# Two transfers of 16 four-byte rows at the head of the load queues, and two weight loads in one piece instead of two

## The chip, the cores and the metric

The kernel runs on one core of one Trainium2 chip. The metric is the device time of one execution in microseconds (us), as the median of several runs. Beside it stands one profiled execution, from which the span (first to last instruction) and all views are taken.

## The reference, cut to what matters

One block of a diffusion transformer with an image stream (2 x 256 tokens) and a text stream (2 x 32 tokens), D = 1152, all in bf16:

```
mod_i = (silu(c) @ wmod_img).reshape(B, 6, 1, D)        # shift, scale, gate; the same for text
shi, sci, gai = mod_i[:, 0], mod_i[:, 1], mod_i[:, 2]
hi   = layernorm(x_img) * (1 + sci) + shi
qkvi = hi @ wqkv_img                                     # q, k, v in thirds of 3*D columns
...
p    = softmax(q @ k.T * D**-0.5)                        # text and image tokens joined, per batch
a    = p @ v
out_i = x_img + gai * (ai @ wo_img)
out_t = x_txt + gat * (at @ wo_txt)
```

## The kernel before, in words

The order of all work is written out by hand (`tc.manual_schedule()`): each engine runs its instructions in program order, and so does each load queue.

**Loads.** Every weight comes from HBM in row tiles of 128 partitions. SyncE's queue (SP, in the profile queue q1) carries nearly all of them, in the order of the program: `c` (L81), then the four column chunks of the image scale weight `w_sc_i` (`load_sc`, L94) with the rows of the image value weight `w_v_i` (`load_v`, L98, L110: nine row tiles `kt`, 288 KB each) and two tiles of `x_img` (`load_x`, L90) between them, and after these the other weights (`load_w`, L76). The first two of the four tiles of `x_img` are issued on ScalarE's queue (ACT, q10). `load_w` takes a tuple `ksplits`: `K3` loads a weight in three pieces, `K2` in two (kt 0 to 4, kt 5 to 8), the default in one piece. Five buffers of the pool `w` go round among the large weights; `w_ga_i` has the home "V", the place that `w_v_i` leaves.

The framework gives every transfer on the two hardware queues one of eight semaphores in turn. A transfer that gets a semaphore again waits at its issue until the one eight places before it has landed.

**First stage (0 to about 31 us).** TensorE runs 15 matmuls on zeros to warm up (L143). Meanwhile VectorE takes the layernorm statistics of x tile 0 (L169), then of tiles 1 and 2. With each scale chunk (two or three kt of columns) TensorE computes the scale columns (`mod_scale`, L223; the last chunk by `mod_scale_last`, L240 and L245), and the value projection accumulates row by row over kt (`v_row`, L282; `v_narrow`, L294) as the scale columns and the value rows arrive. The matmuls of kt 6 to 8 need the last chunk's scale.

**The rest.** The shift row, q and k of the image, the text stream, scores, softmax, attention and the output projections follow, almost without a gap on TensorE. `w_sc_t` (text scale, L460) is read by `row_strips` through `mod_strip` (L429), `w_ga_i` (image gate, L464) by `scores_txt_and_gate` (L636, L641, L657).

**The spare columns.** `xf_full` is a tile of 128 x (2*VC + 64), with VC = 288. Its view `xf` uses columns 0 to 2*VC - 1, loaded late (L812) and read at the end (L879). The columns from 2*VC on are read by nothing.

Of the kernel before, what the change touches and what calls it, by code (L numbers as in the profile page):

```python
# [14 lines left out]
def kernel(  # L15
# [14 lines left out]
    nc = tc.nc  # L30
# [4 lines left out]
    B, NI, D = x_img.shape  # L35
    NT = x_txt.shape[1]
    P = 128
# [7 lines left out]
    VC = 288  # L45
# [18 lines left out]
    xi_flat = x_img.rearrange("b n d -> (b n) d")  # L64
# [5 lines left out]
    def w_view(src):  # L70
        return src.rearrange("(kt p) n -> p kt n", p=P)

    def load_w(src, c0, ksplits=((0, KT),), home=None):
        t = wpool.tile([P, KT, D], bf, tag="w", name="t") if home is None else act.tile([P, KT, D], bf, tag=home, name="w_home")
        for (k0, k1) in ksplits:
            nc.sync.dma_start(t[:, k0:k1, :], w_view(src)[:, k0:k1, c0:c0 + D])  # L76
        return t
# [6 lines left out]
    xf_full = act.tile([P, 2 * VC + 64], bf)  # L84
# [4 lines left out]
    def load_x(i, eng=nc.sync):  # L89
        eng.dma_start(x_i[:, i, :], xi_t[:, i, :])  # L90

    def load_sc(ch):
        k0, k1 = KC[ch]
        nc.sync.dma_start(w_sc_i[:, :, k0 * P:k1 * P], w_view(wmod_img)[:, :, D + k0 * P:D + k1 * P])  # L94
# [4 lines left out]

    for i in range(TPB):  # L100
        load_x(i, nc.scalar)
    load_sc(0)
    load_x(2)
    load_v(0)
# [9 lines left out]
    K2 = ((0, 5), (5, KT))  # L114
# [342 lines left out]

    w_k_i = load_w(wqkv_img, D, K3)
    w_sh_t = load_w(wmod_txt, 0)
    w_sc_t = load_w(wmod_txt, D, K2)  # L460
    nc.sync.dma_start(x_t[0:P:P // NTT, :], xt_flat[:, :])
    w_q_t = load_w(wqkv_txt, 0, K2)
    w_k_t = load_w(wqkv_txt, D, K2)
    w_ga_i = load_w(wmod_img, 2 * D, K2, home="V")  # L464
    w_v_t = load_w(wqkv_txt, 2 * D, K3)
    w_o_i = load_w(wo_img, 0, K2)
    w_ga_t = load_w(wmod_txt, 2 * D)
# [461 lines left out]
```

## Time and profile before

| What | Value |
|---|---|
| median of 3 runs | 114.57 us (114.54 to 114.64) |
| the profiled execution's own time | 114.88 us |
| its span, first to last instruction | 113.1 us |
| TensorE matmul busy | 108.3 us, 96% of the span |
| VectorE, ScalarE, GpSimd busy | 76.1, 36.6, 28.4 us |
| bytes moved | 40.87 MB, mean 361 GB/s |
| mean granted TensorE clock | 0.997 |

The span is 1.78 us shorter than the profiled execution's own time, and that execution is 0.31 us over the median of the runs. A difference that is read from the span is therefore added to the median as it is. TensorE's 96% is an average: which engine or transfer sets the pace has to be read stage by stage.

### The profile page before, as it was taken

The page shows a single profiled execution, that of the slowest core. Times are in us where ns is not written, and L with a number is a line of the kernel's source. Part 1 is how long each engine was busy: PE and PEld are TensorE (multiplying, and loading weights), DVE is VectorE, ACT ScalarE, POOL GpSimd, SP SyncE. Part 2 cuts the span into 40 slices and gives each one's busy share as a digit, 9 for nine tenths or more (in the row PEclk, how much of TensorE's full clock was granted, in tenths as well). Part 3 has the DMA queues.
Part 4 walks back from the last instruction along what each step waited for, and adds up shares of the span by engine and source line. Part 5 has one row for each costly group of instructions (what it writes and reads, how often), then busy time and mean ns, then how long its engine had stood idle before and what let it go on. Part 6 is the DMA issues. An engine that isn't in the chain of part 4 may idle for free.

```text
span 113.1 us, 2863 instructions
## 1 busy us (share of the span) xinstructions
PE 108.3 (96%) x1195; PEld 64.0 (57%) x1204; DVE 76.1 (67%) x151; ACT 36.6 (32%) x83; POOL 28.4 (25%) x65
## 2 busy tenths in 40 slices
PE   5999999999999999999999999999999999999990
PEld 1356655555444444444446558787687556567670
DVE  1699330956399999999999950237666802995971
ACT  4537500372190071740008924025646700001000
POOL 7100120730140000000000060601550470699300
PEclk9999999999999999999999999999999999999998
DMA  3999999999999999999999999999999999994052
GB/s 92 343 333 355 375 375 405 412 411 408 407 412 412 410 411 402 413 410 412 412 411 415 408 405 407 408 392 394 407 411 397 412 408 406 371 375 161 0 191 70
DMA packets 22839, 40.87 MB, mean 361 GB/s; under 512 B 1375, under 2 KB 6635, under 8 KB 22827
## 3 DMA queue, kind: packets, MB, share of 16 engines
q1 hardware_dynamic: 21547, 39.05, 90.4%
q10 hardware_dynamic: 672, 0.77, 2.2%
q0 software_dynamic: 608, 0.88, 2.1%
q8 instruction: 9, 0.15, 0.5%
q14 instruction: 3, 0.02, 0.1%
HBM read 39.36 MB, written 1.34 MB: 360 GB/s over the span
## 4 chain that ended last, share of the span: by engine, by line
PE 80%; DMA 13%; SPq 4%; issue 1%; DVE 0%
PE qkps L529 31%; PE ps L851 16%; DMA w_sc_i<-in_wmod_img_dram 13%; PE va L282 7%; PE aps L759 5%; PE ps L590 4%; PE sps L619 4%; PE gps L429 3%; SPq L98 3%; PE ops L869 2%; PE ps L694 2%; PE van L294 1%; PE gps L824 1%; PE sps L632 1%; PE pk L703 1%
## 5 line engine op out<-in xcount | busy, mean ns | idle before, releaser
L529 PE MATMUL qkps<-hT_i,t 128*128 128x512 bf16 x158 | 35.4, 379 | 0.2
L529 PEld LDWEIGHTS <-t 128*128 128x128 bf16 x162 | 15.6, 98 | 18.7 <-issue 0.4
L491 DVE SCALAR_TENSOR_TENSOR sacc<-w_v_i,mcols,sacc 128x1152 f32<-128x1152 bf16 x16 | 22.7, 1418 | 0.5
L282 PE MATMUL va<-w_v_i,hT_i 128*128 128x512 bf16 x67 | 17.0, 379 | 0.5 <-issue 0.3
L851 PE MATMUL ps<-t,aT 128*128 128x384 bf16 x99 | 16.4, 326 | 0.0
L851 PEld LDWEIGHTS <-aT 128*128 128x128 bf16 x117 | 11.0, 98 | 6.8 <-issue 0.5
L282 PEld LDWEIGHTS <-hT_i 128*128 128x128 bf16 x72 | 6.4, 98 | 6.2 <-issue 0.2
L835 POOL TENSOR_TENSOR w_og<-t,gb 128x384 bf16<-128x384 bf16 x9 | 8.7, 999 | 4.5 <-DMA gb<-mod_scratch 4.5
L857 DVE TENSOR_TENSOR tmp<-ps,gb 128x384 bf16<-128x384 f32 x11 | 6.0, 550 | 5.6 <-DMA gb<-mod_scratch 5.0
L548 POOL TENSOR_SCALAR mod_txt<-mcols 128x18 f32<-128x18 f32 x2 | 0.6, 275 | 32.4 <-DVE mcols L435 32.4
L169 DVE BATCH_NORM_STATS2 stats<-x_i 128x6 f32<-128x384 bf16 x12 | 5.8, 541 | 2.6 <-DMA x_i<-in_x_img_dram 2.6
L143 PE MATMUL wps<-wz 128*128 128x512 bf16 x15 | 6.1, 578 | 1.2 <-DVE wz L125 1.2
L479 ACT ACTIVATE qT<-qkps 128x512 bf16<-128x512 f32 x9 | 4.7, 600 | 6.9 <-PE qkps L529 6.9
L495 ACT CAST shi<-sacc 128x1152 bf16<-128x1152 f32 x2 | 2.3, 1154 | 13.2 <-DVE sacc L491 13.2
L772 DVE TENSOR_SCALAR aT<-aps,sv 128x288 bf16<-128x288 f32 (+2 forms) x11 | 4.3, 455 | 2.0 <-PE aps L759 2.0
L590 PEld LDWEIGHTS <-t 128*128 128x128 bf16 x162 | 5.0, 98 | 0.5
L157 DVE CAST kT<-qkps 128x512 bf16<-128x512 f32 x3 | 2.1, 686 | 4.7 <-PE qkps L529 4.7
L590 PE MATMUL ps<-hT_t,t 128*128 128x64 bf16 x162 | 5.0, 193 | 0.0
L858 DVE TENSOR_TENSOR o<-tmp,x_i 128x384 bf16<-128x384 bf16 x11 | 4.7, 426 | 0.4
L759 PE MATMUL aps<-pT,v_i 128*128 128x288 bf16 (+2 forms) x44 | 4.8, 264 | 0.0
L774 ACT ACTIVATE aT<-aps,sv 128x288 bf16<-128x288 f32 (+2 forms) x11 | 4.0, 468 | 2.1 <-PE aps L759 2.1
L619 PE MATMUL sps<-kT,qT 128*128 128x288 bf16 x36 | 4.6, 286 | 0.0
(160 smaller groups left out, 139.7 us busy)
## 6 DMA issues: line engine op xcount, KB each, us to landing
t<-in_wqkv_img_dram SPq DMA_DIRECT2D x6, 864.0 KB, 13.2
t<-in_wmod_txt_dram SPq DMA_DIRECT2D x2, 2592.0 KB, 17.6
t<-in_wqkv_txt_dram SPq DMA_DIRECT2D x2, 1440.0 KB, 14.2
t<-in_wmod_img_dram SPq DMA_DIRECT2D x3, 864.0 KB, 12.3
t<-in_wqkv_txt_dram SPq DMA_DIRECT2D x3, 864.0 KB, 14.1
t<-in_wo_txt_dram SPq DMA_DIRECT2D x3, 864.0 KB, 15.5
t<-in_wqkv_txt_dram SPq DMA_DIRECT2D x2, 1152.0 KB, 15.0
w_v_i<-in_wqkv_img_dram SPq DMA_DIRECT2D x7, 288.0 KB, 6.9
```

Of the source, the lines that this page charges most:

```text
L143: nc.tensor.matmul(ps[:], lhsT=wz[:, 0:P], rhs=wz[:], start=True, stop=True)
L169: nc.vector.bn_stats(stats[0:np_, k, :], x_ap[:, k * CH:(k + 1) * CH])
L282: nc.tensor.matmul(ps[:], lhsT=hT_i[:, kt, i * P:(i + 1) * P], rhs=w_v_i[:, kt, half * VW:(half + 1) * VW], start=(kt == 0), stop=(kt == K ...
L479: nc.scalar.mul(out_ap, in_ap, SCALE)
L491: nc.vector.scalar_tensor_tensor(saccs[b][:], w_v_i[:, kt, :], ap, saccs[b][:], op0=ALU.mult, op1=ALU.add)
L529: nc.tensor.matmul(pss[j - j0][:], lhsT=wq[:, kt, j * P:(j + 1) * P], rhs=hT_i[:, kt, :], start=(kt == 0), stop=(kt == KT - 1))
L590: nc.tensor.matmul(ps[:, j - j0, :], lhsT=wq[:, kt, j * P:(j + 1) * P], rhs=hT_t[:, kt, :], start=(kt == 0), stop=(kt == KT - 1))
L619: nc.tensor.matmul(sps[:], lhsT=qkTs[0][:, ft, b, q0:q0 + P], rhs=qkTs[1][:, ft, b, :], start=(ft == 0), stop=(ft == KT - 1))
L759: nc.tensor.matmul(bank[:, off:off + c1 - c0], lhsT=lhsT, rhs=rhs, start=(first[id(bank)] == n), stop=(final[id(bank)] == n))
L835: nc.gpsimd.tensor_mul(w_og[:, dt, 0:CH], w_o_i[:, dt, NG0:D], gb[:, B - 1, NG0:D])
L851: nc.tensor.matmul(ps[:, 0:cw], lhsT=aT[:, dt, t0:t0 + P], rhs=rhs, start=(dt == DTS[0]), stop=(dt == DTS[-1]))
L857: nc.vector.tensor_mul(tmp[:, 0:cw], ps[:, 0:cw], gb[:, b, cs])
```

## The change

Two small transfers are added after the first two x tiles. One is on ScalarE's queue and reads the first two elements (4 bytes) of every 16th row of x tiles 2 and 3 (256 rows, so 16 rows). The other is on SyncE's queue, behind `c` and ahead of the first scale chunk, and reads the first two value columns of every 8th row of the first row tile of `wqkv_img` (128 rows, so 16 rows). Both write into columns of `xf_full` that nothing reads. `w_sc_t` and `w_ga_i`, which were loaded in two pieces each, are loaded in one. The number of transfers on the two hardware queues stays the same; two of them move from the middle to the head.

```diff
     for i in range(TPB):
         load_x(i, nc.scalar)
+    nc.scalar.dma_start(xf_full[0:16, 2 * VC + 2:2 * VC + 4], xi_flat[2 * P:4 * P:16, 0:2])
+    nc.sync.dma_start(xf_full[0:16, 2 * VC:2 * VC + 2], wqkv_img[0:P:8, 2 * D:2 * D + 2])
     load_sc(0)
     load_x(2)
     load_v(0)
...
     w_k_i = load_w(wqkv_img, D, K3)
     w_sh_t = load_w(wmod_txt, 0)
-    w_sc_t = load_w(wmod_txt, D, K2)
+    w_sc_t = load_w(wmod_txt, D)
     nc.sync.dma_start(x_t[0:P:P // NTT, :], xt_flat[:, :])
     w_q_t = load_w(wqkv_txt, 0, K2)
     w_k_t = load_w(wqkv_txt, D, K2)
-    w_ga_i = load_w(wmod_img, 2 * D, K2, home="V")
+    w_ga_i = load_w(wmod_img, 2 * D, home="V")
```

## The prediction

> **What bounds the kernel now.** I read the chain of waits first, then the timeline of the first 20 us, then TensorE by stage, then the two load queues in short windows around 3.6 us. The chain, from its start to 32 us:
>
> ```profile
> 0.73 0.41 SPq L81
> 1.14 0.07 issue
> 1.21 5.34 DMA w_sc_i<-in_wmod_img_dram
> ...
> 10.29 8.84 DMA w_sc_i<-in_wmod_img_dram
> 19.14 0.04 issue
> 19.18 0.57 PE sps L245 x36
> ```
>
> Columns are start, length, what. The chain starts on SyncE's queue, at the very place of the edit: issue of c, then the first scale chunk. The last scale chunk lands at 10.29 + 8.84 = 19.13 us, and L245 follows at once. From there on the chain is TensorE without a break. So a microsecond by which the last chunk lands later is paid in full at the end. TensorE by stage (start:end and length, PE busy, count, clock, DMA share, GB/s):
>
> ```profile
> 8.99:11.10 2.11, 2.06 (x15) 1.00 1.08 367
> 11.10:12.84 1.74, 1.71 (x34) 1.00 1.10 353
> 12.84:19.18 6.34, 6.23 (x55) 1.00 1.07 391
> 19.18:31.35 12.17, 11.80 (x141) 1.00 1.04 409
> 31.35:110.00 78.65, 78.44 (x907) 1.00 0.97 375
> ```
>
> TensorE is busy almost throughout from 8.99 us. A faster DMA stream has little to give; the wait that it could shorten is the one ahead of L245, and the timeline prices it:
>
> ```profile
> 18.89 0.23 PE L240 MATMUL sps<-ones_full 128*32 128x96 bf16 x4
> ...
> 19.18 0.20 PEld L245 LDWEIGHTS <-sT 128*32 128x32 bf16 x15 [0.18 <-issue]
> ```
>
> The weight loads of L245 sat 0.18 us: that is all there is to win at this place. The stage that ends here starts from x tile 0:
>
> ```profile
> 0.73 0.41 SPq L81 DMA_DIRECT2D c<-in_c_dram  x1
> 0.74 0.87 ACTq L90 DMA_DIRECT2D x_i<-in_x_img_dram  x2
> 1.21 0.42 SPq L94 DMA_DIRECT2D w_sc_i<-in_wmod_img_dram  x1
> ...
> 3.80 1.48 DVE L169 BATCH_NORM_STATS2 stats<-x_i 128x6 f32<-128x384 bf16 x3 [2.64 <-DMA x_i<-in_x_img_dram]
> ```
>
> VectorE waits for that tile and then hardly pauses until it feeds the first transposes; TensorE's value matmuls start at 9.05. That the x tile isn't loaded sooner therefore matters as much as the last chunk.
>
> **The added transfer on SyncE.** The nearest row for its issue is c, also a small transfer: 0.41 us, and 1.21 - 0.73 = 0.48 us from start to start. So the first scale chunk is issued 0.48 us later, and behind it x tile 2, the value rows and the later chunks, all on that queue. Are they covered? Later on, yes. Issues from 3.82 us on are held back by a queue that is full (two value loads take 2.49 us to issue there, 3.27 us at 6.98), and DMA is at 0.99 to 1.15 of its capacity in every window of 1 us from 5 to 19 us. A later issue costs nothing while transfers issued earlier keep the engines busy. At the head there is nothing issued earlier but the two x tiles on q10. The queues from 2.9 to 3.6 us, then from 3.6 to 4.07 us (packets, MB, share of 16 engines):
>
> ```profile
> q10 hardware_dynamic: 115, 0.24, 96.4%
> q1 hardware_dynamic: 10, 0.01, 2.4%
> ```
>
> ```profile
> q1 hardware_dynamic: 202, 0.10, 72.5%
> q10 hardware_dynamic: 39, 0.06, 32.6%
> ```
>
> Up to 3.6 us the x tiles fill the engines alone; at 3.6 us the first chunk takes over as they run out. The chunk comes when the cover ends. Bounds for the loss: nothing, if its descriptors lay ready at the engines long before and only waited behind x; all of 0.48 us, if the engines stand still for the whole shift. Between them: in the 0.47 us from 3.6 the chunk used 72.5% of the engines, 0.47 x 0.725 = 0.34 us of full DMA time, and x the rest. With the chunk shifted by that much, x still runs and the 0.34 us is lost. I take **+0.34**: 10 packets of the chunk among 115 of x from 2.9 to 3.6 say that it was only just arriving, on a few engines, and was not lying ready.
>
> The Trainium skill, in "DMA: Bandwidth & Descriptors" (Specifications), gives some 0.6 us from the issue to the first byte on the hardware queues; by that the chunk, issued by 1.63, would be there at 2.2, and 0.48 us more would still be covered by x. The trace doesn't agree: packets of 512 bytes hardly flow before 3.6. By the page the term is 0 instead of 0.34.
>
> **The packets themselves.** From 4.07 to 5.3 us, q1 ran 777 packets, mostly of 512 bytes, at a share of 107.1%: 1.23 x 16 x 1.071 / 777 = 27 ns each. A 4-byte packet is at most about that. If the 16 rows are spread over 16 engines, each transfer puts one data and one completion packet on each: four in all, 0 to 0.11 us; I take **+0.04**. If one engine got all 16 rows, 16 x 27 = 0.43 us on it, which the other engines' work would mostly hide.
>
> **What reading early could save.** x tile 2 and value rows 0 and 1 go from 5.3 to 7.9 us: 0.89 MB at 341 GB/s. Value rows of the same shape run at 410 GB/s from 12.9 to 14.3. At that rate 0.89 MB takes 2.17 instead of 2.6 us: 0.43 us is lost, two thirds of it, 0.29, in the two tiles that the new transfers touch. If the loss is a cost of the first touch, up to 0.29 us (0.43 with row 1) comes back. Against it: the first scale chunk is a first touch as well and runs at 323 GB/s with the engines full (4.07 to 5.3), while the later chunk mixed in from 8.6 to 10.4 gives 337. A first touch isn't slower there. I take a third, **-0.10**.
>
> **The added transfer on ScalarE.** A third issue like the two of 0.87 us: 0.44 us. Behind it on that engine stands its table load (1.64, 1.28 us long), which then ends near 3.36 instead of 2.92; SiLU runs at 3.26 now, so it slips by 0.1 us. What needs it first is the scale matmul at 7.00. On q10 the packets are behind both x tiles. Cost 0.
>
> **The two merged loads.** Same bytes, same rows. The pieces of `w_sc_t` are issued at 32.3 and 38.2 us and the reader, L429, runs from 60.6; `w_ga_i` is issued at 59.6 and 60.0, lands 11.5 to 14.0 us later, so by 74.0, and is first read at 78.7. TensorE must now wait for whole tiles, but they are whole 4.7 us ahead; without that cover it would be the second piece's 2.9 us. The semaphore turn shifts by two at the head and is back after the merges. Value row 1 (issued at 2.86) now waits for x tile 0 (about 3.8), yet its bytes flow only after 6.4. Cost 0.
>
> **Sum.** 0.34 + 0.04 - 0.10 = **+0.28 us**. The profiled execution would go from 114.88 to 115.16, its span from 113.1 to 113.4, the median from 114.57 to **114.85**.
>
> **Rivals.**
>
> *Hidden anyway.* The descriptors of the first chunk lie ready, the shift is covered by x; stalls saved are worth at most what L245 waits. -0.18 to +0.11: 114.39 to 114.68, likeliest 114.57. For it: DMA never falls below capacity after 2.5 us. Against it: the 10 packets above. In "DMA: Bandwidth & Descriptors", the section that issuing engines aren't separate DMA queues, the Trainium skill says that sequencer time is usually small beside the transfer; that would be this case.
>
> *First touch pays.* The slow start of x tile 2 and value rows 0 and 1 is a first-touch cost, and the new reads take it while the engines have room (DMA share 0.50 from 1.5 to 2.0 us, 0.70 to 2.5, full only then). The stream gains 0.29 to 0.43. It decides as soon as the gain exceeds the 0.34 + 0.04 lost at the head, or all of it if that is hidden. TensorE can take 0.18 at L245, more only where runs without a profile wait longer there. Time 114.57 - 0.29 = 114.28. For it: x tiles 0 and 1 also start slowly (101 GB/s up to 2.9 us). Against it: the scale chunk's row, and TensorE's full stages.
>
> *The cold read delays x tile 0.* The 16 value rows are read while x tile 0 is on the same engines. If a first read holds an engine, VectorE's start at 3.80 moves. The price is bounded by the same slow stretch: 0.43 us over about three transfers, 0.14 each. With the sum above 114.85 + 0.14 = 114.99. Against it: the new packets are on another ring than x.
>
> **How the numbers follow.** 0.2%, 0.23 us, is about what a measurement of this kernel can tell from no change. Forecast (+0.28) 0.46, cold read as well 0.09, hidden 0.27, first touch 0.18. Slower by over 0.2%: 0.55. Faster by over 0.2%: 0.17, nearly all of first touch. Within: 0.28. The range goes from 114.28, where first touch pays, to 114.57 + 0.48 = 115.05, where the whole issue is exposed. The forecast's own range is 114.69 to 115.05.
>
> **What would show it.** The first chunk issued near 1.69; few q1 packets up to 4.0 and a dip of the DMA share at 3.6 to 4.1; L245 near 19.5, with a longer idle time before its weight loads; all later TensorE stages of the same length. Value rows 0 and 1 at 341 GB/s would show no first-touch gain; over 380, one. Wrong if L245 starts at 19.2 or sooner, or if VectorE's first statistics move from 3.80.

## The result and the profile after

The changed kernel takes 115.16 us (median of 21 runs, 114.70 to 115.69); the kernel before, run beside it, 114.64 us (21 runs, 114.46 to 115.01). The ratio is 1.004 with a 95% interval of 1.003 to 1.005: slower by 0.34 to 0.57 us. The profiled execution takes 115.15 us, its span is 113.4 us, against 114.88 and 113.1.

The head of the changed kernel in order of time (start, length, engine, line, tiles, idle time before and what ended it):

```profile
1.20 0.32 SPq L103 DMA_DIRECT2D xf_full<-in_wqkv_img_dram  x1
1.57 0.42 SPq L94 DMA_DIRECT2D w_sc_i<-in_wmod_img_dram  x1
...
3.77 1.48 DVE L171 BATCH_NORM_STATS2 stats<-x_i 128x6 f32<-128x384 bf16 x3 [2.61 <-DMA x_i<-in_x_img_dram]
...
7.16 0.60 PE L225 MATMUL mps<-sT,w_sc_i 128*128 128x2 bf16 x18 [0.83 <-DMA w_sc_i<-in_wmod_img_dram]
...
9.02 1.89 PE L284 MATMUL va<-w_v_i,hT_i 128*128 128x512 bf16 x7
...
19.24 0.41 PEld L247 LDWEIGHTS <-sT 128*32 128x32 bf16 x35 [0.26 <-issue]
```

The same places in the kernel before (its warm-up, first scale matmul, first value matmuls):

```profile
3.16 4.22 PE L143 MATMUL wps<-wz 128*128 128x512 bf16 x11
...
7.21 0.59 PE L223 MATMUL mps<-sT,w_sc_i 128*128 128x2 bf16 x18
...
9.05 1.89 PE L282 MATMUL va<-w_v_i,hT_i 128*128 128x512 bf16 x7
```

The first chunk is issued at 1.57 instead of 1.21. VectorE starts when it did (3.77). What is new is the idle time of TensorE ahead of the first scale matmul: 0.83 us, ended by the first chunk. Before, the trace shows no wait for a transfer there, only TensorE's own warm-up, which took longer: the 11 warm-up matmuls from 3.16 us take 4.22 us before and 3.16 us here. Yet in this execution the value matmuls start at 9.02, as before (9.05), and the last chunk's matmul (L247, which was L245) at 19.24 instead of 19.18. From there to VectorE's last addition it is 91.22 us, before 91.20. So this one execution shows 0.06 us at the place where the prediction looked. The other 0.2 us of the longer span lies behind that addition, in the last stores and the closing barrier, in which the engines wait for one another. The last addition, before and changed (start, length, what):

```profile
110.38 0.29 DVE o L854
```

```profile
110.46 0.29 DVE o L856
```

From its end to the end of the span (113.10 and 113.38 us) it is 2.43 us before and 2.62 us here. That stretch is called the closing below; it turns out to be the steadier part of the loss. For the head one trace is too little: single executions of either kernel spread over half a microsecond or more.

The queues in the two windows of the prediction, 2.9 to 3.6 and 3.6 to 4.07 us (packets, MB, share of 16 engines):

```profile
q10 hardware_dynamic: 115, 0.24, 101.0%
q1 hardware_dynamic: 24, 0.00, 2.1%
```

```profile
q1 hardware_dynamic: 130, 0.07, 51.1%
q10 hardware_dynamic: 51, 0.09, 47.5%
```

In the second window q1 falls from 72.5 to 51.1%, but q10 takes 47.5 instead of 32.6%: the engines together stay at 98.6%. In this window the shift of the issue left hardly a hole in the stream: 0.47 x (1.051 - 0.986) = 0.03 us, not the 0.34 forecast. A dip comes later, from 6 to 7 us: 0.91 of the engines instead of 0.99, 0.08 us.

### The profile page after: what moved, and what is told of

It reads as the page before. It is cut to its first block, busy times and chain, and to the rows that moved or that the text cites. A ratio compares the mean times of both kernels' runs of the same rounds, so it can differ in the third digit from the quotient of the medians.

```text
span 113.4 us, 2862 instructions
## 1 busy us (share of the span) xinstructions
PE 107.4 (95%) x1195; PEld 63.6 (56%) x1204; DVE 75.7 (67%) x151; ACT 36.6 (32%) x83; POOL 28.4 (25%) x65
## 3 DMA queue, kind: packets, MB, share of 16 engines
HBM read 39.36 MB, written 1.34 MB: 359 GB/s over the span
## 4 chain that ended last, share of the span: by engine, by line
PE 80%; DMA 10%; SPq 6%; issue 1%; DVE 0%
PE qkps L531 31%; PE ps L853 16%; DMA w_sc_i<-in_wmod_img_dram 7%; PE va L284 7%; SPq L98 5%; PE aps L761 5%; PE ps L592 4%; PE sps L621 4%; PE gps L431 3%; DMA x_i<-in_x_img_dram 3%; PE ops L871 2%; PE ps L696 2%; PE van L296 1%; PE gps L826 1%; PE sps L634 1%
## 5 line engine op out<-in xcount | busy, mean ns | idle before, releaser
L145 PE MATMUL wps<-wz 128*128 128x512 bf16 x15 | 5.0, 494 | 1.2 <-DVE wz L127 1.2
```

The costliest lines, as they stand in the source:

```text
L145: nc.tensor.matmul(ps[:], lhsT=wz[:, 0:P], rhs=wz[:], start=True, stop=True)
```

## The experiments

Theory A after this trace: the issue ahead of the first chunk is what costs, by the landing of that chunk. Rivals: B, the first read of untouched rows holds single engines; C, the merged loads or the new semaphore turn; D, ScalarE's transfer. In each comparison the kernel before ran beside the others on the same chip; ratios are against it, with 95% intervals. In what follows, "small transfer" is one of the two that the change adds. None of these kernels changes the computation.

### The parts alone

Only the merges:

```diff
-    w_sc_t = load_w(wmod_txt, D, K2)
+    w_sc_t = load_w(wmod_txt, D)
...
-    w_ga_i = load_w(wmod_img, 2 * D, K2, home="V")
+    w_ga_i = load_w(wmod_img, 2 * D, home="V")
```

> The two weight loads in one piece each, neither small transfer. All theories that put the loss at the head (the issue on SyncE's queue, a read that holds engines while the x tiles come) expect no change: 114.6, within 0.1 of before, L245 at 19.1 to 19.2. The rival that the merges cost something in the middle (whole tiles waited for, another semaphore turn) expects 114.8 to 115.1, with TensorE idle at 60 or 79 us.

Measured: 1.0000 (0.9983 to 1.0017). C falls for the merges; this kernel has two transfers fewer, so it doesn't test the new turn.

Only SyncE's transfer, with `w_sc_t` in one piece:

```diff
+    nc.sync.dma_start(xf_full[0:16, 2 * VC:2 * VC + 2], wqkv_img[0:P:8, 2 * D:2 * D + 2])
     load_sc(0)
...
-    w_sc_t = load_w(wmod_txt, D, K2)
+    w_sc_t = load_w(wmod_txt, D)
```

> Only the small transfer on SyncE's queue (value rows), and w_sc_t in one piece so that the number of transfers stays. If the loss is the issue ahead of the first chunk or the first read of the value rows: most of the 0.5 us, 115.0 to 115.2, first chunk issued at 1.57. If the small transfer on ScalarE's queue is what costs: within 0.1 of before. Value rows 0 and 1 should flow without the slow packets (near 390 GB/s).

Measured: 1.0013 (0.9989 to 1.0036). Not settled, and repeated later:

> SyncE's small transfer alone, repeated, since the first time gave +0.11 with an interval that held everything. If the issue ahead of the chunk is paid in full whatever else is there: +0.35 to +0.5. If the chunk has some slack up to the 7.1 us at which TensorE first takes it, and it needs both transfers to use it up: 0 to +0.2, the chunk's last engine landing below 7.1.

Measured: 1.0016 (0.9993 to 1.0040). Twice below the changed kernel's 1.004, and both intervals reach 1. Their upper ends, 0.41 and 0.46 us, would still allow the whole 0.36 us by which the chunk is issued later; the medians say that a part of it is paid.

Only ScalarE's transfer, with `w_sc_t` in one piece:

```diff
+    nc.scalar.dma_start(xf_full[0:16, 2 * VC + 2:2 * VC + 4], xi_flat[2 * P:4 * P:16, 0:2])
     load_sc(0)
...
-    w_sc_t = load_w(wmod_txt, D, K2)
+    w_sc_t = load_w(wmod_txt, D)
```

> Only the small transfer on ScalarE's queue (x rows of tiles 2 and 3), and w_sc_t in one piece. Theory of the SyncE issue: within 0.1 of before (114.6), first chunk issued at 1.21. Rival, the read of the x rows ahead of the chunk on the engines stalls it: 114.9 to 115.2, with the first chunk landing after 6.8 instead of 6.5.

Measured: 1.0005 (0.9987 to 1.0023). D falls as the cause of the whole loss.

The changed kernel once more, beside merge_only, the first SyncE run and this one:

> The changed kernel once more, for a second trace and as the control of the other three: 115.0 to 115.3 against 114.6. The first trace shows L247 only 0.06 later than before and 0.17 in the closing barrier; if the loss is in the head, this trace should show more of it there, the chunk landing near 7 and the last chunk's landing moving with the slowest engine.

Measured: 1.0023 (1.0003 to 1.0043), median 115.15 against 114.78: slower again. Its trace (same columns as above) shows what the first one only hinted at:

```profile
1.56 0.42 SPq L94 DMA_DIRECT2D w_sc_i<-in_wmod_img_dram  x1
...
7.78 0.38 SPq L94 DMA_DIRECT2D w_sc_i<-in_wmod_img_dram  x1
7.81 0.60 PE L225 MATMUL mps<-sT,w_sc_i 128*128 128x2 bf16 x18 [1.34 <-DMA w_sc_i<-in_wmod_img_dram]
...
9.28 1.89 PE L284 MATMUL va<-w_v_i,hT_i 128*128 128x512 bf16 x8
```

The first chunk lands near 7.8: both the scale matmul and the issue of the third chunk, which waits for the first chunk's semaphore, come then. The value matmuls now start at 9.28. The slack between the chunk and VectorE's chain, which the first trace still had, is used up and 0.26 us of the stage is gone. The last chunk's matmul starts at 19.19 all the same, as in the trace of before (19.18), where it was the last chunk that came late; the closing is 2.61 us again.

### Issue or first read

The changed kernel with other rows in the small transfers, rows that are loaded at the head anyway:

```diff
-    nc.scalar.dma_start(xf_full[0:16, 2 * VC + 2:2 * VC + 4], xi_flat[2 * P:4 * P:16, 0:2])
-    nc.sync.dma_start(xf_full[0:16, 2 * VC:2 * VC + 2], wqkv_img[0:P:8, 2 * D:2 * D + 2])
+    nc.scalar.dma_start(xf_full[0:16, 2 * VC + 2:2 * VC + 4], xi_flat[0:2 * P:16, 0:2])
+    nc.sync.dma_start(xf_full[0:16, 2 * VC:2 * VC + 2], c.rearrange("b (kt p) -> (b kt) p", p=P)[0:16, 0:2])
```

> The changed kernel, but the small transfers read rows that are loaded at the head anyway: SyncE's reads 16 rows of c, ScalarE's every 16th row of x tiles 0 and 1. Issues, packets and semaphore turn stay. Theory that the loss is the issue and the packets: as the changed kernel, +0.3 to +0.5, the first chunk's last engine landing at 7.1 or later. Rival that first reads of untouched rows hold single engines: within 0.1 of before, the chunk landing near 6.7.

Measured: 1.0022 (1.0004 to 1.0039), close to the changed kernel's 1.0023 in the comparison before. No effect of the rows is seen, but the two intervals leave room for a difference of some 0.2 us, and this one begins at +0.05 us: B isn't settled by this run, and a gain of 0.1 us from reading early is too small for it. The next two kernels decide B better: they read the same untouched rows without the loss.

The changed kernel with SyncE's transfer behind the chunk:

```diff
-    nc.sync.dma_start(xf_full[0:16, 2 * VC:2 * VC + 2], wqkv_img[0:P:8, 2 * D:2 * D + 2])
     load_sc(0)
+    nc.sync.dma_start(xf_full[0:16, 2 * VC:2 * VC + 2], wqkv_img[0:P:8, 2 * D:2 * D + 2])
     load_x(2)
```

> The changed kernel with SyncE's small transfer behind the first scale chunk instead of ahead of it; all else stays. Theory of the issue ahead of the chunk: the chunk is issued at 1.21 again, 0.3 to 0.5 comes back, within 0.1 of before or as with ScalarE's transfer alone (+0.07). Rival, the read itself (wherever it is) or the semaphore turn: +0.3 or more stays.

Measured: 1.0001 (0.9981 to 1.0020). x tile 2, the value rows and the second chunk are still issued later, the semaphore turn behind the chunk is the changed kernel's, the closing too (2.61 us), and no loss is seen. What differs from the changed kernel is the first chunk's place:

```profile
1.21 0.42 SPq L94 DMA_DIRECT2D w_sc_i<-in_wmod_img_dram  x1
...
7.55 0.59 PE L225 MATMUL mps<-sT,w_sc_i 128*128 128x2 bf16 x18
...
9.01 1.89 PE L284 MATMUL va<-w_v_i,hT_i 128*128 128x512 bf16 x7
```

The scale matmul waits for no transfer here.

The changed kernel with both on ScalarE's queue (`nc.sync` of the second line made `nc.scalar`), and the repetition:

> The changed kernel with both small transfers on ScalarE's queue behind the x tiles. Theory of the issue on SyncE: as ScalarE's transfer alone, +0.0 to +0.15. Rival, that the reads disturb the stream while the chunk starts, whichever queue has them: +0.3 to +0.5.

> Both small transfers on ScalarE's queue, repeated: the first time 0.9988 of before, interval 0.9975 to 1.0002. If the reads ahead are worth something once they cost no issue on SyncE: 0.1 to 0.2 faster again. If not: within 0.1 of before. In either case the first chunk is issued at 1.20.

Measured: 0.9988 (0.9975 to 1.0002) and 0.9991 (0.9979 to 1.0002). The loss is gone. Both medians are below before (114.60 against 114.77, 114.56 against 114.62), but each interval just reaches 1: a gain of 0.1% is not established, nor is it excluded. The closing is 2.42 us in both traces, so about 0.2 us of the difference to the changed kernel is won there and not at the head.

The Trainium skill, in "DMA: Bandwidth & Descriptors" (section on issuing engines not being separate DMA queues), says that another issuing engine saves only the sequencer's time, usually small beside the transfer. The first half agrees: the queue was changed, and the first chunk is issued 0.36 us sooner. So does the second, as 0.36 us is small beside the 5.34 us from the chunk's issue to its landing. Small isn't free, though, where it stands ahead of the transfer that TensorE needs first.

One more small transfer on SyncE's queue, ahead of the chunk, added to the changed kernel:

```diff
     nc.sync.dma_start(xf_full[0:16, 2 * VC:2 * VC + 2], wqkv_img[0:P:8, 2 * D:2 * D + 2])
+    nc.sync.dma_start(xf_full[0:16, 2 * VC + 4:2 * VC + 6], c.rearrange("b (kt p) -> (b kt) p", p=P)[0:16, 0:2])
     load_sc(0)
```

> The changed kernel with one more small transfer (16 rows of c) on SyncE's queue ahead of the chunk. Theory of the issue: the chunk is issued 0.36 later again, near 1.92, lands near 7.5 or later, past the 7.1 at which TensorE can first use it, so every further 0.36 is paid: +0.65 to +0.9 in all. Rival of the cold reads: no more than the changed kernel, +0.3 to +0.5.

Measured: 1.0078 (1.0056 to 1.0100), twice the loss or more:

```profile
1.56 0.41 SPq L104 DMA_DIRECT2D xf_full<-in_c_dram  x1
2.02 0.42 SPq L94 DMA_DIRECT2D w_sc_i<-in_wmod_img_dram  x1
...
7.78 0.49 PEld L226 LDWEIGHTS <-w_sc_i 128*128 128x128 bf16 x17 [0.66 <-DMA w_sc_i<-in_wmod_img_dram]
...
9.26 1.89 PE L285 MATMUL va<-w_v_i,hT_i 128*128 128x512 bf16 x7
...
12.07 0.60 PE L226 MATMUL mps<-sT,w_sc_i 128*128 128x2 bf16 x18 [0.56 <-DMA w_sc_i<-in_wmod_img_dram]
```

The first chunk holds TensorE to 7.78. Here the second chunk too is late: its scale matmul, at 11.23 before, starts at 12.07 after 0.56 us of waiting. But theory A can't claim all of it: the closing is 2.93 us here, 0.5 us more than before, and that is half of the 0.90 us lost. SyncE's waits for the last stores, before and here (us in total, times, longest):

```profile
SPq L924 <- DMA out_dram<-o: 0.6, 2, 0.4
```

```profile
SPq L927 <- DMA out_dram<-o: 1.1, 1, 1.1
```

This kernel has one transfer more than the others, so the turn of the eight semaphores ends at another one: SyncE now waits for the last store before it checks the other semaphores, and not behind most of them. That is rival C, at the end of the kernel. Without the closing 0.4 us is left.

The same two on SyncE's queue without ScalarE's transfer, both loads in one piece:

> Two small transfers (value rows, c) on SyncE's queue ahead of the chunk, none on ScalarE's. Issue paid in full: as the run with three small transfers, +0.8 to +0.95. Slack first: the first 0.36 hidden, the second paid, +0.3 to +0.6. If ScalarE's transfer is what makes the engines late: +0.1 or less.

Measured: 1.0024 (0.9995 to 1.0054). Between the expectations of "slack first" and nothing; its interval holds both. It excludes the third: the chunk is issued 0.82 us later (2.03), and at most 0.62 us is lost. The closing is 2.45 us, as before, so here the loss of about 0.28 us is the head's. In its trace the scale matmul starts at 7.98, the value matmuls at 9.45.

One row instead of 16 in SyncE's transfer (`xf_full[0:1, ...]`, `wqkv_img[0:1, ...]`, the rest as changed):

> The changed kernel, but SyncE's small transfer moves one row of 4 bytes instead of 16. Theory of the issue: its length hardly changes (about 0.32), so the loss stays, +0.25 to +0.5. Rival that packets on all 16 engines hold them up: within 0.1 of ScalarE's transfer alone (+0.07).

Measured: 1.0010 (0.9981 to 1.0039), median 115.19 against 114.83. The median agrees with the changed kernel, the interval with nothing lost: inconclusive on whether packets on 16 engines add to the issue. The issue is shorter than expected, 0.23 us instead of 0.32, and the chunk is issued at 1.48.

### Is the chunk a limit before as well?

The kernel before with c moved, so that the first chunk is issued at 0.73: once behind the chunk on SyncE's queue, once on ScalarE's queue between the x tiles.

```diff
-    nc.sync.dma_start(c18[:], c.rearrange("b (kt p) -> (b kt) p", p=P))
...
     load_sc(0)
+    nc.sync.dma_start(c18[:], c.rearrange("b (kt p) -> (b kt) p", p=P))
```

> The kernel before, with c issued behind the first scale chunk instead of ahead of it; the chunk is issued 0.47 earlier, near 0.73. If the chunk's landing sets the start of TensorE's work in most executions, this is faster, -0.1 to -0.45. If VectorE's chain from x tile 0 (9.0 us) is as late, the chunk is only a limit when it is delayed: within 0.1 of before, or slower by what the later c delays the warm-up.

Measured: 1.0273 (1.0226 to 1.0320), 3.2 us slower.

```diff
-    for i in range(TPB):
-        load_x(i, nc.scalar)
+    load_x(0, nc.scalar)
+    nc.scalar.dma_start(c18[:], c.rearrange("b (kt p) -> (b kt) p", p=P))
+    load_x(1, nc.scalar)
```

> The kernel before, with c issued on ScalarE's queue between x tiles 0 and 1; the first chunk is issued near 0.73. If the chunk's landing limits the kernel before in many executions: -0.1 to -0.3. If VectorE's chain limits it: within 0.1; slower by 0.1 to 0.4 if x tile 1 or the later c become the limit.

Measured: 1.0222 (1.0196 to 1.0247), 2.6 us slower. Neither expectation held. The trace of the second says why:

```profile
0.73 0.44 SPq L93 DMA_DIRECT2D w_sc_i<-in_wmod_img_dram  x1
1.21 0.79 ACTq L100 DMA_DIRECT2D c<-in_c_dram  x1
...
4.83 1.48 DVE L169 BATCH_NORM_STATS2 stats<-x_i 128x6 f32<-128x384 bf16 x3 [3.67 <-DMA x_i<-in_x_img_dram]
5.93 0.19 PE L149 MATMUL cT_ps<-ident,c 18*128 18x18 bf16 x1 [2.83 <-DMA c<-in_c_dram]
6.05 4.87 PE L143 MATMUL wps<-wz 128*128 128x512 bf16 x11
...
10.72 0.66 PE L223 MATMUL mps<-sT,w_sc_i 128*128 128x2 bf16 x18
```

In this kernel x tile 0 comes about 1 us later (4.83 against 3.80), x tile 1 3 us later (its statistics at 8.45 against 5.46), and c at 5.93 instead of 3.03. TensorE's warm-up matmuls stand in program order behind c and then run to 10.7; VectorE's chain from x tile 1 is about as late. In the other kernel x tile 0 is only 0.14 us later (3.94) and c alone is the limit: it comes at 6.61, and the first scale matmul starts at 11.16, behind the warm-up. The head is tight on both sides: the chunk ahead of x and c costs more than the chunk behind a small transfer. Whether an earlier chunk alone would help is left open by these two, since both made c late.

### Two more traces

> Third trace of the changed kernel. First chunk issued at 1.56, last engine landing at 7.1 to 7.8; TensorE's first scale matmul after it. L245 at 19.2 or later, either because the stage started late (value matmuls after 9.1) or because the last chunk lands late. The theory of the first chunk says the former, the theory of the whole stream the latter.

> Second trace of the kernel before. First chunk issued at 1.21, last engine landing at 6.3 to 6.8, value matmuls at 9.0, L245 at 18.8 to 19.2.

Measured, single executions: 114.75 us for the changed kernel, 114.95 for before. The third trace of the changed kernel is one in which the chunk was in time:

```profile
6.77 0.60 PE L225 MATMUL mps<-sT,w_sc_i 128*128 128x2 bf16 x18 [0.46 <-DMA w_sc_i<-in_wmod_img_dram]
...
8.97 1.89 PE L284 MATMUL va<-w_v_i,hT_i 128*128 128x512 bf16 x7
```

Over the traces a rule shows. Where the first scale matmul started by 7.6 us and x tile 1 was there, the value matmuls started at 8.97 to 9.05. Where the first chunk was later, they start 1.47 us behind that matmul: 7.81 and 9.28, 7.79 and 9.26, 7.98 and 9.45. Of nine traces with a small transfer ahead of the chunk, four have the late start because of it; a fifth, one row on SyncE's queue, starts at 9.82, but there x tile 1 was late and explains that by itself. Of the seven of other kernels with the chunk issued near 1.2 us, none starts late because of the chunk. The chunk's landing says the same: 6.2 to 7.2 us in those seven, 6.7 to 8.2 in the seven in which it was issued near 1.5, 7.7 and 7.9 in the two in which it was issued at 2.0.

| Kernel | Chunk issued | First scale matmul | Value matmuls | Last chunk's matmul | Closing | Profiled time |
|---|---|---|---|---|---|---|
| before | 1.21 | 7.21 | 9.05 | 19.18 | 2.43 | 114.88 |
| before, second | 1.20 | 7.49 | 8.98 | 19.21 | 2.46 | 114.95 |
| value rows behind chunk | 1.21 | 7.55 | 9.01 | 18.81 | 2.61 | 114.56 |
| changed | 1.57 | 7.16 | 9.02 | 19.24 | 2.62 | 115.15 |
| changed, second | 1.56 | 7.81 | 9.28 | 19.19 | 2.61 | 115.17 |
| changed, third | 1.57 | 6.77 | 8.97 | 18.87 | 2.61 | 114.75 |
| SyncE alone, second | 1.56 | 7.79 | 9.26 | 19.93 | 2.47 | 115.64 |
| two on SyncE, none on ScalarE | 2.03 | 7.98 | 9.45 | 19.35 | 2.45 | 114.94 |
| one more on SyncE | 2.02 | 7.79 | 9.26 | 19.58 | 2.93 | 115.65 |

Three things move the time. Two act through the last chunk's matmul: a late start of the stage, and the last chunk's own landing, which scatters in both kernels (19.18 and 19.21 before, with the stage on time). The third is the closing, and it hardly scatters: traces of one kernel agree within 0.03 us. It goes with the number of transfers that SyncE issues. Where SyncE issues as many as before (50), the closing is 2.43 to 2.47 us in six traces. Where it issues one fewer, as in the changed kernel, it is 2.61 to 2.63 in all eight. With two fewer it is 2.42 twice (both on ScalarE's queue) and 2.55 (merges alone). Only the kernel with one transfer more in all (2.93) stands apart. Why a single issue fewer lengthens the closing, the traces don't show.

How the loss splits is an estimate. From the last chunk's matmul to the profiled time it is 95.70 and 95.74 us before, 95.91, 95.98 and 95.88 in the changed kernel. Taken from the medians (114.64 and 115.16), that puts this matmul at 18.92 and 19.24 in the median execution: some 0.3 us are lost ahead of it and some 0.2 behind it, nearly all in the closing. The kept traces don't show the 0.3 by themselves: both traces of before are slower than its median. Nor do the times of the other kernels confirm the share of the closing: ScalarE alone and value rows behind the chunk have the long one too and lose nothing that can be seen (1.0005 and 1.0001, each with some 0.2 us either way), so either their intervals hide it or they win as much elsewhere. How much of the 0.3 is the late start and how much the last chunk's landing is open.

## Why the prediction was wrong

It said slower, +0.28 us, 114.85, and a range up to 115.05. Measured were 115.16, and +0.46 by the ratio. The direction was right, and so was one of the two places, the issue ahead of the first chunk: behind the chunk, with all else the same, the small transfer cost nothing that can be seen (1.0001).

**The step that failed** is the top of the range and of the sum: 0.48 us, "where the whole issue is exposed", was taken for all that can be lost. The stages behind the last chunk were to keep their length, and the end of the kernel stood in no term, without a reason. TensorE's stages did keep their length; the closing didn't. It takes 2.61 or 2.62 us in all three traces of the changed kernel and 2.43 and 2.46 in both of before: some 0.17 us, seen in the profiled executions, at which the prediction put nothing. What had been counted was the transfers on both queues together, which stay the same, and not SyncE's, which fall by one. Another 0.07 us of the miss is the start: the kernel before took 114.64 beside the changed one, not 114.57. That 0.28 + 0.17 = 0.45 comes so near to the measured 0.46 is partly luck, as the terms of the 0.28 show:

- **"I take +0.34"** came near to the 0.3 estimated for the head, for a wrong reason. It counted a hole in the whole stream, carried to the last chunk. The engines had hardly any hole there (98.6% in the window), and a later stream behind the chunk shows no cost (1.0001). What the traces show is the first chunk itself: TensorE idles for it (0.83 and 1.34 us), and when it comes after some 7.6 us the value matmuls move with it. The prediction named 7.00 only as the time when SiLU's result is needed; it did not list the first chunk's landing, in a chain it had printed (1.21 + 5.34 = 6.55), against the time when its reader could use it.
- **"I take a third, -0.10"** isn't shown and isn't refuted. The kernel with both transfers on ScalarE's queue, which reads the same rows early without delaying the chunk, has medians 0.17 and 0.06 us below before, with intervals that just reach 1; a gain of 0.1 us is below what these comparisons resolve. The sign that the prediction named, the rate of the value rows, couldn't have told. In its window from 5.3 to 7.9 us the changed kernel has 337 GB/s, no more than the 341 before; with the merges alone, and no early read, one execution has 380. So the rate changes from one execution to the next. The time of the rival "first touch pays", 114.28, did not come.
- **The bounds, nothing to 0.48 us,** of one linear term aren't refuted for the head. Without the closing the losses by the ratios are 0.15 and 0.18 us for SyncE's transfer alone, 0.28 for two of them, 0.42 for these two and ScalarE's. With a shift of 0.36 and 0.82 us, that agrees with a cost of a little less than half the shift, and also with a slack that is used up first; the intervals of some 0.2 us either way don't tell the two apart.
- **"Cost 0" for ScalarE's transfer** holds for it alone within the interval (1.0005), though the closing is 2.62 us there too. Whether it adds to SyncE's at the head stays open: the intervals overlap.
- **"Cost 0" for the merges** holds (1.0000).
- **The rival "hidden anyway"** is what SyncE's transfer alone nearly does. The 0.6 us to the first byte of the Trainium skill ("DMA: Bandwidth & Descriptors", Specifications) would have made the term 0; the changed kernel lost some 0.3 us at the head by the estimate.
- **"The cold read delays x tile 0"** fell: VectorE's first statistics start at 3.72 to 3.77 in the three traces of the changed kernel.
- **The issue** took 0.32 us, not 0.41, so the chunk stands at 1.57 instead of 1.69. L245's place was forecast at 19.5; it came at 19.24, 19.19 and 18.87, two of three times below the 19.2 that the prediction had named as a sign of being wrong.

## What to carry to other kernels

At the head of a kernel, before any backlog exists, list for the first few transfers when each lands and when its reader could first use it; an issue put ahead of one of them delays that landing, and what this costs depends on the slack. The same small transfer one place later, or on another engine's queue, showed no loss. Where executions spread over half a microsecond, one profile of each kernel doesn't show a change of 0.4: compare landmarks over several traces. Take the end of the kernel as one of them, also for a change at its start: here some 0.2 us of the loss were there, and an experiment with one transfer more seemed to confirm the theory of the head with 0.5 us that belonged to the closing.

## What was not expected of the hardware

- A small transfer issued second at the head comes much later: c, issued 0.48 us later (1.21 instead of 0.73) behind x tile 0 and beside a chunk issued first, was there at 5.93 instead of 3.03 us.
- The closing of the kernel changed with a single transfer: 2.43 to 2.47 us with 50 issues on SyncE's queue, 2.61 to 2.63 with 49, and 2.93 with one transfer more in all.
- An issue of 16 rows of 4 bytes takes 0.32 us of SyncE's queue and 0.45 us of ScalarE's, one of a single row 0.23 us of SyncE's; the scale chunk, with 1152 rows of 512 bytes, takes 0.42.
- The same warm-up of 11 matmuls on zeros took 3.16 us in one trace and 4.22 us in another, at a granted clock of 1.00 in both stretches. Where it ends late, the traces show no wait for a first chunk that landed before its end.
